# Storing each output tile by one transfer of 128 lanes in place of two of 64

## The chip, the cores and the metric

The kernel runs on one core of one Trainium2 chip. The metric is the device time of one execution in microseconds (us), the median of the runs shown. A profile of one execution on the chip, with its trace, was taken of the kernel before.

## The reference

Cosine attention over 8 batches, 12 heads, 448 positions and a head size of 64, and then a highway layer over the 3584 tokens of 768 numbers that come out of it. Inputs and output are float32.

```python
# q, k, v: (8, 12, 448, 64); tau = 0.1; w_h, w_t: (768, 768); b_t: (768,)
q_n = q / (norm(q, axis=-1) + 1e-6)
k_n = k / (norm(k, axis=-1) + 1e-6)
scores = q_n @ k_n^T / tau
attn = softmax(scores)
x = (attn @ v).transpose(0, 2, 1, 3).reshape(3584, 768)
H = maximum(x @ w_h, 0)
T = sigmoid(x @ w_t + b_t)
out = T * H + (1 - T) * x
```

## The kernel before, in words

**Layout.** The 448 positions of a batch are written as 64 lanes l by 7 positions j, position = 7 l + j (`(l j)` with `NJ = 7`). The two halves of the 128 lanes of a tile hold two different values of something: two heads of a pair in q and k, and two neighbouring j in x and in the output. The tile `x` of a batch is [128 lanes, 7, 384] and holds the attention's result in fp16.

**Attention.** For each batch, q and k are loaded (`ld_qk`, q from the SP queue at L321 and L323, k from POOL), squared (L388) and summed for the norms, scaled (`scale`, L440, mostly on POOL), and turned so that the head size lies on the lanes: by TensorE (L455) in the early batches, and by DMA transposes on SP in the later ones (q from batch 3 on at L457, k from batch 5 on at L463). `scores` makes the products (L504, L515) and their exponentials on ACT (L510, L517); `attend` multiplies by v (L529, L534, L542) and DVE divides by the sums into `x` (L550).

**Highway layer.** `ffn(b, i)` handles one of four tiles of a batch, numbered g = 4 b + i. Tiles i = 0, 1, 2 hold 128 rows of 768 numbers: lanes 0 to 63 are the rows with j = 2 i, lanes 64 to 127 those with j = 2 i + 1. The tile i = 3 (the tail) holds j = 6 alone: its 64 rows are cut into two halves of 384 numbers, one on each half of the lanes. The tile of x is turned (from batch 1 on by a DMA transpose on SP, L670, into one of five `xT` buffers), multiplied with both weights (L690, for the tail L687), put through the bias (L719), the gate (L732, L734), the product with the gate, and the last sum (L760, on POOL for most tiles), which writes the float32 tile `os`. There are four `os` buffers. `store` then writes it to the output from SP, at L770 for a whole tile and at L767 for a tail. The last two tiles (g = 30 and 31, `late`) have a path of their own with stores at L750 and L752, one half from SP and one from ACT.

**Order.** Nothing is scheduled at run time. Each piece of work is an `op` with an engine, the names that it reads, writes and uses; `ORDER` is a list of the 1911 operation numbers in the order in which they are given out, and each engine runs its own operations in that order. `SLOTS` says for each ring of buffers which buffer each new tile takes. So SP runs 109 operations in a fixed row: q loads (`ldq`), transposes of x (`xd6`, `xd3`), q (`xd7`) and k (`xdk`), and stores (`st`). One operation `st` issues two transfers. An operation that waits (a store for its `os` tile, a transpose for its source) holds all that comes behind it on SP.

Of the kernel before, what the change touches and what calls it, by code (L numbers as in the profile page):

```python
# [93 lines left out]
""".split()  # L94
)

SLOTS = {
    "qr": "01010101",
    "kr": "0120121",
    "kn": "012012012012120120120120",  # L100
    "vr": "01010101",
    "vp": "01010101",
    "sq": "012102102121021021021201012201010221021201210102",
    "n2": "01010101",
    "y": "01201201",
    "tu": "01010101010",
# [93 lines left out]
def kernel(  # L200
# [11 lines left out]
    nc = tc.nc  # L212
# [663 lines left out]
```

## Time and profile before

| what | us |
|---|---|
| median of 3 runs (lowest 250.49, highest 251.38) | 250.71 |
| profiled execution, its own time | 251.74 |
| span of the profiled execution, first to last instruction | 250.0 |
| TensorE busy (matmuls) in the span | 232.6 |
| ACT busy | 211.0 |
| DVE busy | 205.2 |
| POOL busy | 183.7 |

The profile is of one execution. Its page lists each engine's busy time, the span in 40 slices (busy tenths of each engine and of the 16 DMA engines, and the GB/s that they moved), the DMA queues (q1 is SP's, q0 is POOL's, q10 is ACT's), the chain of work that ended last, the costliest groups of instructions, and the DMA issues by tile with their size and the median time from issue to landing. A group is named by line, engine and tiles, as in "L770 SPq DMA_DIRECT2D out_dram<-os". "SPq" is SP's sequencer, which issues transfers; its issue time is not the time that the transfer takes. "DMA share" is the mean busy share of the 16 DMA engines over a stretch; it can pass 1, since the records of two queues on one engine may overlap.

### The profile page before, as it was taken

To read this page: it belongs to the slowest core of one execution; us is meant where nothing else is said; L and a number is where in the kernel's file an instruction comes from. 1 tells how busy PE (TensorE), PEld (TensorE's weight loads), DVE (VectorE), ACT (ScalarE), POOL (GpSimd) and SP (SyncE) were. 2 spreads that over 40 slices of the span, in tenths; PEclk is the share of its full clock that TensorE was granted. 3 is DMA by queue.
4 is the path that set the end of the run, shared out by engine and by line. 5 is a ranking of instruction groups with operands and counts; after the bars stand their busy time and mean duration, and the time that the engine had idled before them with its cause. 6 is when DMAs were issued, how large, how long until landed. Compare 5 with 4: busy or idle time off the path is not lost.

```text
span 250.0 us, 7394 instructions
## 1 busy us (share of the span) xinstructions
PE 232.6 (93%) x2856; PEld 147.4 (59%) x2856; DVE 205.2 (82%) x462; ACT 211.0 (84%) x421; POOL 183.7 (73%) x261
## 2 busy tenths in 40 slices
PE   7668899999999999999999999999999799999990
PEld 2246676566765765657566566656565456575650
DVE  6777899999999899999899875899974564766993
ACT  4588999999999999999999999999999399652320
POOL 8476689989989979898679778779489940334550
PEclk9855999999999999999999999999999999999996
DMA  7999999999779999999899997999996978458475
GB/s 229 296 229 271 302 248 210 198 224 210 112 132 268 167 155 239 177 134 277 257 143 175 213 151 144 247 250 161 143 174 133 181 149 185 82 143 173 121 186 157
DMA packets 75924, 47.78 MB, mean 191 GB/s; under 512 B 51568, under 2 KB 72688, under 8 KB 75888
## 3 DMA queue, kind: packets, MB, share of 16 engines
q1 hardware_dynamic: 55584, 33.86, 62.1%
q0 software_dynamic: 19856, 12.68, 39.0%
q10 hardware_dynamic: 448, 0.75, 0.9%
q8 instruction: 22, 0.36, 0.6%
q14 instruction: 14, 0.11, 0.1%
HBM read 38.34 MB, written 11.01 MB: 197 GB/s over the span
## 4 chain that ended last, share of the span: by engine, by line
PE 65%; ACT 18%; DVE 3%; DMA 3%; issue 2%; SPq 0%; DVEq 0%; ACTq 0%
PE B L690 32%; ACT E L510 10%; PE B L504 8%; PE B L534 7%; PE B L687 4%; ACT sq L388 3%; PE B L529 3%; DMA kT<-kn 3%; PE B L515 2%; PE B L455 2%; PE B L542 2%; ACT Et L517 2%; ACT E L594 2%; ACT tt L732 1%; PE B L608 1%
## 5 line engine op out<-in xcount | busy, mean ns | idle before, releaser
L510 ACT ACTIVATE E<-B 128x448 f16<-128x448 f32 x252 | 122.9, 634 | 4.6 <-PE B L504 4.5
L690 PEld LDWEIGHTS <-xT 128*128 128x128 f16 x576 | 52.6, 98 | 37.3 <-issue 7.3
L760 POOL TENSOR_TENSOR os<-x,hm 128x384 f32<-128x384 f16 x53 | 47.6, 912 | 31.5 <-DVE hm L755 19.6
L690 PE MATMUL B<-wt,xT 128*128 128x384 f16 x288 | 56.5, 326 | 0.1
L440 POOL TENSOR_TENSOR kn<-kr,y 128x192 f16<-128x192 f16 (+1 forms) x84 | 45.5, 561 | 14.7 <-DVE hm L755 6.6
L690 PE MATMUL B<-wh,xT 128*128 128x384 f16 x288 | 55.7, 326 | 0.1
L399 DVE TENSOR_REDUCE n<-sq 128x14 f32<-128x896 f32 (+1 forms) x50 | 51.1, 1037 | 3.4 <-ACT sq L388 3.2
L440 POOL TENSOR_TENSOR qn<-qr,y 128x448 f16<-128x448 f32 x47 | 43.9, 940 | 5.0 <-ACT sq L388 2.4
L732 ACT ACTIVATE tt<-z 128x768 f16<-128x768 f32 (+1 forms) x32 | 26.5, 830 | 15.9 <-DVE z L719 15.9
L534 PE MATMUL B<-vp,E 128*128 128x65 f16 x756 | 37.7, 193 | 0.0
L728 DVE SCALAR_TENSOR_TENSOR hm<-B,x 128x384 f16<-128x384 f32 x53 | 28.2, 549 | 10.2 <-PE B L690 5.5
L534 PEld LDWEIGHTS <-E 128*128 128x128 f16 x756 | 33.4, 97 | 3.0
L504 PE MATMUL B<-qT,kT 64*128 64x448 f16 x252 | 34.2, 353 | 0.0
L517 ACT ACTIVATE Et<-B 128x448 f16<-128x448 f32 x42 | 26.2, 643 | 3.6 <-PE B L515 3.5
L529 PE MATMUL B<-vp,Et 128*128 128x130 f16 x126 | 28.0, 222 | 0.0
L719 DVE TENSOR_TENSOR z<-B,bias 128x384 f32<-128x384 f32 x48 | 25.8, 545 | 2.4 <-PE B L690 2.1
L550 DVE SCALAR_TENSOR_TENSOR x<-B,rd 128x448 f16<-128x448 f32 x42 | 25.8, 618 | 0.8
L388 ACT ACTIVATE sq<-qr 128x896 f32<-128x896 f32 (+1 forms) x24 | 24.3, 1045 | 0.7 <-DMA qr<-in_q_dram 0.7
L344 POOL DMA_DIRECT2D vr<-in_v_dram x32 | 22.2, 701 | 0.1
L594 ACT ACTIVATE E<-B 128x384 f16<-128x384 f32 (+1 forms) x42 | 20.2, 644 | 1.2 <-PE B L587 1.1
L549 DVE RECIPROCAL rd<-B 128x7 f32<-128x7 f32 x42 | 8.2, 198 | 14.9 <-PE B L534 8.2
L388 ACT ACTIVATE sq<-kr 128x896 f32<-128x896 f16 x17 | 17.0, 1052 | 0.0
(79 smaller groups left out, 306.4 us busy)
## 6 DMA issues: line engine op xcount, KB each, us to landing
out_dram<-os SPq DMA_DIRECT2D x47, 192.0 KB, 3.4
qr<-in_q_dram SPq DMA_DIRECT2D x6, 1344.0 KB, 8.4
kr<-in_k_dram POOLq DMA_DIRECT2D x7, 672.0 KB, 7.9
vr<-in_v_dram POOLq DMA_DIRECT2D x16, 192.0 KB, 6.4
vr<-in_v_dram POOLq DMA_DIRECT2D x16, 144.0 KB, 6.5
qr<-in_q_dram SPq DMA_DIRECT2D x5, 448.0 KB, 7.9
out_dram<-os SPq DMA_DIRECT2D x15, 96.0 KB, 2.3
wt<-in_moe_w_t_dram POOLq DMA_DIRECT2D x1, 1152.0 KB, 13.8
```

Source lines behind the costliest of these rows:

```text
L388: nc.scalar.activation(dst, src, AF.Square, scale=sc)
L399: nc.vector.reduce_sum(R("n2", b)[:, c : c + 7 * n], a, axis=AX.X)
L440: ENG[eng].tensor_mul(N[:, :, t, :] if nm == "q" else N[:, lo > 0 : (lo > 0) + 2 * (hi - lo) - 1 : 2, t, :], source(nm, b, g)[:, t, 64 * l ...
L504: nc.tensor.matmul(R("B", ("S", n, c, t))[:, 0:S], lhsT=R("kT", i)[ln, s, 128 * c : 128 * c + 128], rhs=queries(ln), start=True, stop=True)
L510: nc.scalar.activation(R("E", n)[:, at : at + 7, :].rearrange("l j x -> l (j x)"), R("B", ("S", n, c, t))[:, 0:S], AF.Exp)
L517: op("ACT", f"expt {n}", lambda: nc.scalar.activation(R("Et", n).rearrange("l j x -> l (j x)"), R("B", ("St", n))[:, 0:S], AF.Exp), r=[("B ...
L529: nc.tensor.matmul(U[:, 2 * c : 2 * c + 2, :], lhsT=Et[:, 2 * c : 2 * c + 2, :].rearrange("l j x -> l (j x)"), rhs=vp[:, 6:8, 0:65], start ...
L534: nc.tensor.matmul(U[:, 2 * c + t, :], lhsT=E[:, at : at + 2, :].rearrange("l j x -> l (j x)"), rhs=vp[:, 3 * t + m, 0:65], start=False, s ...
L690: nc.tensor.matmul(P[:, 0:MH], lhsT=xT[:, cc, :], rhs=w_[:, cc, MH * mh : MH * mh + MH], start=(cc == 0), stop=(cc == CC - 1))
L728: op("DVE", f"hm {g} {mh}", lambda at=at, sl=sl, mh=mh: nc.vector.scalar_tensor_tensor(out=R("hm", g)[:, sl], in0=R("B", at)[:, 0:MH], sca ...
L732: op("ACT", f"th{nb} {g}", lambda: nc.scalar.activation(R("tt", g)[:, 0:W], R("z", g)[:, 0:W], AF.Tanh, scale=0.5), r=[("z", g), ("t0",)], ...
L760: op(eng, f"out {g} {mh}", lambda sl=sl, mh=mh: ENG[eng].tensor_add(R("os", g)[:, sl], xpart(mh), R("hm", g)[:, sl]), r=[("gg", g), xk], w ...
```

## The change

`store` issues one transfer for a tile in place of two. For a whole tile, the destination is both j together, `rows[2 * i : 2 * i + 2]`, whose three dimensions are j, l and m, and the source all 128 lanes. For a tail, the destination is the 64 rows with their two halves of 384 numbers put first. `rows` is a view of the output in the order j, l, m.

```diff
         def store():
             rows, O = out[b * S : b * S + S].rearrange("(l j) m -> j l m", j=NJ), R("os", g)
             if tail:
-                for h in range(2):
-                    nc.sync.dma_start(rows[6, :, MH * h : MH * h + MH], O[64 * h : 64 * h + 64, 0:MH])
+                nc.sync.dma_start(rows[6].rearrange("l (h m) -> h l m", h=2), O[:, 0:MH])
             else:
-                for h in range(2):
-                    nc.sync.dma_start(rows[2 * i + h], O[64 * h : 64 * h + 64, :])
+                nc.sync.dma_start(rows[2 * i : 2 * i + 2], O[:, :])
         op("SP", f"st {g}", store, r=[("os", g)], w=[("o", g)])
```

The two lists are exchanged as well, `ORDER` and ten of the rings of `SLOTS`. The operations and their number are the same. On SP, 16 of the 109 operations stand elsewhere, by one or two places; on PE 280 of 669, by at most 8; on ACT 163 of 425, by at most 7; on DVE 98 of 452 and on POOL 85 of 256, by at most 4. The first line of each list shows the kind of difference:

```diff
 ORDER = tuple(
...
-1 7 30 28 6 4 27 31 20 13 32 29 12 0 36 37 38 302 10 3 2 33 305 35 308 48 25 44 15 34 42 46 19 49 45 309 9 16 43 47 58
...
+30 6 7 28 4 1 27 31 20 32 29 37 36 38 302 0 3 2 33 305 35 308 48 44 34 42 46 19 49 45 309 9 16 43 47 10 58 13 12 25 15
...
```

The path of the last two tiles (`late`) stays as it was.

More of the change, by code (lines that the diff above doesn't have):

```diff
@@ L99 @@
     "kr": "0120121",
-    "kn": "012012012012120120120120",
+    "kn": "012012012012120120120102",
     "vr": "01010101",
     "vp": "01010101",
-    "sq": "012102102121021021021201012201010221021201210102",
+    "sq": "012102102121021020120210102211010221020212021210",
     "n2": "01010101",
@@ L109 @@
     "kT": "01230123013201302130213",
-    "E": "012012012012012020102012010201020120210210210210201210120",
-    "Et": "012021102101210210210210201020210102120210",
-    "rd": "010010101010101011010101010101010101010101010101010010",
+    "E": "012012012012012021012102101210121021201210210210201210120",
+    "Et": "012021102101210210210210210121201012021201",
+    "rd": "010100101010101010101010101010101010101010101010101101",
     "x": "012012012",
-    "xT": "01234012340124310234103241203214",
-    "z": "01001010101010010011010101000101",
-    "tt": "01001010101010101011010010101011",
+    "xT": "01234012340124310234103241203210",
+    "z": "01010101010101101100101010111010",
+    "tt": "01001010101010101011001101010100",
     "hm": "01210120210120121012001201210210",
-    "os": "01231020212101013213230201321023",
+    "os": "01231020212010103203213230120321",
     "B": (
-        "0123456701234567012345601273512463057134025347061351674326513027356473103247065213465072615342054627"
-        "6534207124310564516725340127632174063415602734167301243605172430547126724031547320423146750325610764"
-        "1230571640532146507314625702675013461045214736241370645320716572430173567215036504237012365714032675"
-        "1405416723504501605243676543025620154736017524315704327610534716230547603127530716452610437125604712"
-        "0562571034650731764025372146305430176451302740563270172365170345167302163540317564236147350621305276"
-        "4315362407315645123406172136504137260714356217406"
+        "0123456701234567012345670123570234567124705234716231720657316405627136243071452063403675012345620453"
+        "7421503652460176147351260453760325467231460572345674053267150436740512516034715630163412570364720572"
+        "1360451723406527413074163526513270450127620345620431351064721637540236413721064105367027541325067431"
+        "2650156340721054670512434012570375061423651740271652043671503674502317420653706251473165426371054630"
+        "5173160524716470620453165704123012764301725432760541254607135427130451673425730642174203745612573014"
+        "2656240173652415206174230625471620317240651374021"
     ),
```

144 rows, old and new, of the table ORDER are left out of this document.

## The prediction

> **What bounds the kernel now.** I read the page first: its span, the busy shares, the slices, the DMA queues and the chain.
>
> ```profile
> span 250.0 us, 7394 instructions
> PE 232.6 (93%) x2856; PEld 147.4 (59%) x2856; DVE 205.2 (82%) x462; ACT 211.0 (84%) x421; POOL 183.7 (73%) x261
> DMA  7999999999779999999899997999996978458475
> GB/s 229 296 229 271 302 248 210 198 224 210 112 132 268 167 155 239 177 134 277 257 143 175 213 151 144 247 250 161 143 174 133 181 149 185 82 143 173 121 186 157
> q1 hardware_dynamic: 55584, 33.86, 62.1%
> q0 software_dynamic: 19856, 12.68, 39.0%
> q10 hardware_dynamic: 448, 0.75, 0.9%
> PE 65%; ACT 18%; DVE 3%; DMA 3%; issue 2%; SPq 0%; DVEq 0%; ACTq 0%
> ```
>
> TensorE is busy for 93% of the span and carries 65% of the chain; the sequencer SP, which issues the stores, carries 0%. That is the first reading: a store is off the path, and fewer store issues can hardly buy anything. The second reading is the DMA line: in most slices the sixteen DMA engines are at seven to nine tenths or more, though they move only 112 to 302 GB/s. These engines are shared by everything, and nearly full as an average. So the question that decides is not how many transfers are issued but how evenly the bytes lie on the sixteen engines.
>
> Next, the issues by tile, to see what the changed lines do and when.
>
> ```profile
> L770 SPq DMA_DIRECT2D out_dram<-os x46: 467/588/1392, 74.9 to 243.6; - x46
> L767 SPq DMA_DIRECT2D out_dram<-os x14: 541/582/598, 99.1 to 230.5; - x14
> DMA to landing us min/median/max: 2.2/3.2/8.5
> out_dram<-os SPq DMA_DIRECT2D x47, 192.0 KB, 3.4
> out_dram<-os SPq DMA_DIRECT2D x15, 96.0 KB, 2.3
> qr<-in_q_dram SPq DMA_DIRECT2D x6, 1344.0 KB, 8.4
> ```
>
> L770 issues 46 halves of whole tiles, 192 KB each, and L767 14 halves of tail tiles, 96 KB each: 23 whole tiles and 7 tails, the first at 74.9 us. The last two tiles (L752, L750) are not touched.
>
> **The change, part by part.**
>
> *Issues.* Thirty of the 60 issues at 0.588 and 0.582 us go: 30 x 0.587 = 17.6 us of SP's time. SP is on no share of the chain, so I cost this at nothing; what it could be worth at most is the first rival.
>
> *What one transfer now looks like.* Before, both sides of a store count 64 lanes first: 64 rows of 3072 bytes, lane after lane in the tile, 21,504 bytes apart in the output. After, the tile side counts 128 lanes, but the output side cannot: lanes 0 to 63 go to rows of j = 2i and lanes 64 to 127 to the same rows of j = 2i + 1, and j steps by 3072 bytes where l steps by 21,504. So the 128 rows are no single series; the destination is two halves of 64, the halves outermost. The tails are alike (two halves of 64 rows of 1536 bytes, 1536 bytes apart). The q load looks like a counter-example, since its source is also written with a two outermost (s = 2), and it lands 1344 KB in 8.4 us, which no two engines could do: 1344 KB / 8.4 us = 164 GB/s. It isn't one: its s step is 64 times its l step (448 rows of 64 numbers against 7 of them), so those lanes do fold into one series of 128. Every transfer of the profile that I followed in the code counts 64 or 128 first on both sides. No row shows an outermost count under sixteen, so the cost is bounded from both sides: spread over sixteen engines as now, it is nothing or a small gain; shared out by the halves, one engine takes one half, and two engines carry all the output of 30 tiles. I take two engines, because the halves are the only outer count in which lanes of the tile and rows of the output agree without cutting a half. The Trainium skill says this outright: in "DMA: Bandwidth & Descriptors", section "Why a DMA increments its semaphore by 16 and not by 1", the number of engines is the largest up to 16 that divides the slowest dimension of both access patterns, which would be 2 for 128 and 2, and 16 for the 64 and 64 of before. The q load's 164 GB/s agrees with it, as its folded 128 gives 16; the case of 2 is shown by no row here.
>
> *The price on an engine.* A whole tile puts 64 rows of 3072 bytes, 0.1966 MB, on each of the two engines; a tail half that.
>
> ```profile
> core 0: us, PE busy (x) PEld busy (x) DVE busy (x) ACT busy (x) POOL busy (x), PEclk, DMA share, GB/s
> 75.00:208.00 133.00, 131.00 (x1609) 81.34 (x1606) 110.82 (x244) 126.50 (x258) 107.73 (x153) 1.00 1.10 186
> 208.00:250.00 42.00, 35.75 (x378) 22.52 (x375) 28.46 (x67) 17.09 (x33) 14.21 (x16) 0.95 0.64 152
> 235.30:235.60 0.30, 0.30 (x4) 0.17 (x3) 0.30 (x1) 0.00 (x0) 0.30 (x2) 1.00 1.08 420
> ```
>
> The last row is a piece in which a store alone runs on full engines: 420 GB/s at a share of 1.08 is 420 / (16 x 1.08) = 24.3 GB/s for one engine. The q10 row of the page, loads and the last stores with the pauses between, gives 0.75 MB in 0.9% of 16 x 250 us = 36 us, or 20.8. Two engines with 64 rows queued on each are full, so the 420 row is nearest: 0.1966 MB / 24.3 GB/s = 8.1 us for a whole tile and 4.05 for a tail, where the store now lands in 3.4 and 2.3. At 20.8 it would be 9.45 and 4.7. The ends of the rate are 20.8 and 26.2 (420 / 16, not divided by the share).
>
> *The sum.* These stores do not spread over the run. The timeline of SP shows where they bunch:
>
> ```profile
> 207.96 2.50 SPq L770 DMA_DIRECT2D out_dram<-os  x4
> 210.56 2.90 SPq L670 DMA_TRANSPOSE xT<-x  x2
> 213.51 1.22 SPq L767 DMA_DIRECT2D out_dram<-os  x2
> 219.34 3.18 SPq L770 DMA_DIRECT2D out_dram<-os  x4
> 223.35 3.87 SPq L670 DMA_TRANSPOSE xT<-x  x3
> 227.28 1.22 SPq L767 DMA_DIRECT2D out_dram<-os  x2
> 228.59 1.19 SPq L770 DMA_DIRECT2D out_dram<-os  x2
> 229.88 1.18 SPq L767 DMA_DIRECT2D out_dram<-os  x2
> 231.16 1.24 SPq L670 DMA_TRANSPOSE xT<-x  x1
> 232.50 11.71 SPq L770 DMA_DIRECT2D out_dram<-os  x10
> ```
>
> From 208 us on there are 2 + 2 + 1 + 5 = 10 whole tiles and 3 tails; before it 13 and 4. Up to 75 us nothing changes: 75 us. From 75 to 208 the two engines must do the stores, 13 x 8.1 + 4 x 4.05 = 121.5 us, and their sixteenth of all else. All else is 186 GB/s x 133 us = 24.7 MB, less 13 x 0.393 + 4 x 0.197 = 5.9 MB of stores, so 18.8 MB, 1.18 MB for one engine. Its rate lies between that of the two large queues together (46.5 MB in 101.1% of 4000 us, 11.5 GB/s) and that of q1 alone (33.86 MB in 62.1%, 13.6 GB/s); at 12.5 it is 94 us. That stage takes 215 us in place of 133 if the two engines never pause. From 208 us the stores are 10 x 8.1 + 3 x 4.05 = 93 us and all else 152 x 42 = 6.4 MB less 5.1 MB of stores (the last two tiles' among them), 0.08 MB for one engine, 6 us: 99 us in place of 42. With about 3 us until the last lands, as now (3.4), the two engines alone need 75 + 215 + 99 + 3 = 392 us.
>
> They will pause. What waits behind a store: in SP's queue the DMA transposes of xT, qT and kT and the q loads, which need all engines and so also these two; on SP itself the next store, which waits for its tile; on POOL the sum of L760, which waits for one of four `os` buffers, and behind it the scaling of the next batch's q and k (L440), which SP transposes. If nothing of a store's 8.1 us lay beside other work, the middle stage would take its 133 us plus 121.5 less what its stores cost now on sixteen engines (5.9 MB / 16 / 24.3 = 15 us), 239 us. That is 24 us over 215; four `os` buffers let two or three tiles queue while TensorE goes on, so I take a third, 8 us. 400 us of span. The profiled execution took 251.74, 1.74 outside its span, and lies 1.03 above the median of 250.71: 400 + 1.74 - 1.03 = 401 us.
>
> *The new order.* The lists are written anew: PE's and ACT's operations trade places with near neighbours, 16 of SP's 109 move by one or two. The instructions stay the same, so the busy times stay; it moves waits in both directions, within the 17 us in which PE isn't busy (250.0 - 232.6), most of which lie at the start and end. I take nothing, within 2.5 us either way.
>
> **The rivals.**
>
> *Spread over sixteen engines after all*, by folding inside the hardware or because the lowering cuts the transfer in two again. Then only SP's time falls, and it decides where a transpose waits behind stores. The chain shows one such place:
>
> ```profile
> 191.50 0.53 SPq L457
> 192.09 6.41 DMA kT<-kn
> kT<-kn SPq DMA_TRANSPOSE x18, 4.7
> ```
>
> A kT that lands at its median saves 6.41 - 4.7 and at most the issue before it, 0.53: 2.2 us, so 248.5 us, or nothing if the transfer is cut again, 250.7. For it: 0.59 us for an issue is real, and SP issues two for each tile. Against it: the destination doesn't fold. The Trainium skill speaks for it as well, on the same page, section "Rules for kernel authors": two transfers to disjoint halves of the lanes share the same engines anyway, and one of 128 lanes is advised. Which of the page's two rules wins is the case's question; the destination's halves settle it for me. Chance 0.10: 0.05 for the gain, 0.04 for no change, 0.01 for a small loss by the new order.
>
> *Two engines, and no overlap at all*: each store holds up all that comes behind it, SP's transposes first, so TensorE stands still for each. The middle stage is then the 239 us from above, and the last one 42 + 93 less the 12 us that its stores cost now (4.5 MB / 16 / 24.3), 123: 75 + 239 + 123 = 437 us of span, 438 us. With 20.8 in place of 24.3 the three terms are 75, 257 and 137, which makes 470. It decides if a transpose is needed sooner behind a store than 8 us after its issue; they land in 4.7 us and the chain has 3% of DMA waits now, so some are. Chance 0.2.
>
> *Two engines, but less to carry*: at 26.2 GB/s and with all else at 13.6 GB/s and no pauses, 75 + (113 + 86) + (86 + 6) + 3 = 369 us. It is the lower end of the forecast.
>
> **How the numbers follow.** Two engines with most of the overlap, 369 to 430 us: 0.70, and the likeliest is 401. No overlap: 0.20, 430 to 470. Sixteen engines: 0.10, about 250. The range from 368 to 466 leaves out the sixteen and the far end of the second case, under 2 in 10. About 0.5% can be told from no change here: faster 0.05, same 0.04, slower 0.91.
>
> **What would show it.** Right: 23 issues of 384 KB and 7 of 192 KB, landing in over 8 and 4 us, most of them far more behind one another; slices in which only stores run fall to about 50 GB/s (2 x 24.3) at a DMA share of about one tenth (2 of 16); the DMA `out_dram<-os` and DMA transposes have a large share of the chain and PE falls under 60% of the span with the same busy time, though its granted clock may fall in the pauses; the last transposes issue after 290 us and the end is a run of stores. The packets keep number and size: the q1 row keeps its bytes and grows in packets only by what completions differ. Wrong: stores that land in about 3.4 us, or a last stage that still moves 150 GB/s, mean that the engines are shared out otherwise, and the time is then about that of before. If the time is slower but under 368 us, the two engines carry less than I gave them; if it is over 466, the transposes' waits, not the engines, set the pace.

## The result and the profile after

The changed kernel takes 395.19 us (median of 6 runs, 394.0 to 396.39) against 250.54 us (6 runs): a ratio of 1.5775, 95% interval 1.5744 to 1.5806. The profiled execution took 394.75 us with a span of 393.0 us. The prediction was 401 us, range 368 to 466. In what follows, where the runs of one kernel lay over 1.5% apart (n8 and the two merged ones from POOL's queue), the time given is the median of the faster ones.

The page of the changed kernel, in the parts shown of before: span, engines, granted clock, slices of the DMA engines, SP's queue, the chain and the store's own rows.

```profile
span 393.0 us, 7325 instructions
PE 263.5 (67%) x2856; PEld 160.2 (41%) x2856; DVE 206.6 (53%) x462; ACT 213.8 (54%) x421; POOL 183.9 (47%) x261
PEclk9659999999869897879959995895967977786555
DMA  9999999889999798994969999959795919222131
GB/s 238 258 246 233 206 203 188 125 209 79 71 176 147 105 62 77 234 100 88 63 121 210 113 70 82 148 64 90 112 91 75 64 56 74 71 56 72 52 87 44
q1 hardware_dynamic: 54684, 33.86, 63.5%
DMA 43%; PE 17%; ACT 13%; POOL 7%; SPq 5%; issue 4%; DVE 1%; DVEq 0%; POOLq 0%; ACTq 0%
DMA out_dram<-os 31%; ACT E L510 7%; PE B L690 7%; DMA qr<-in_q_dram 4%; DMA xT<-x 3%; DMA qT<-qn 3%; PE B L504 3%; POOL os L760 3%; ACT sq L388 2%; SPq L457 2%; SPq L463 2%; POOL kn L440 2%; PE B L534 2%; ACT E L594 2%; DMA kT<-kn 1%
out_dram<-os SPq DMA_DIRECT2D x23, 384.0 KB
out_dram<-os SPq DMA_DIRECT2D x8, 192.0 KB
```

The engines' work is the same in count, and DVE's, ACT's and POOL's busy times moved by under 3 us. TensorE's rose by 31 us, which comes up again below; the rest is time around the work. TensorE, 65% of the chain before, has 17%, and the store alone has 31%; it was not on the chain of before. Two readings say how many engines carry a store. First, q1 moves the same 33.86 MB, but in 900 packets fewer, 54684 for 55584. Two transfers on sixteen engines end with 32 completion packets; if one transfer on k engines ends with k, 30 tiles save 30 x (32 - k), and 900 gives k = 2. (The runs below bear the counting out: n4 has 54744 packets, 30 x 28 fewer, and n8 54864, 30 x 24 fewer.) Second, a stretch near the end in which nothing but stores is in flight, below the two stages in which the prediction made its sum (columns: the stretch, busy time and instructions of each engine, granted clock, share of the sixteen DMA engines, GB/s):

```profile
core 0: us, PE busy (x) PEld busy (x) DVE busy (x) ACT busy (x) POOL busy (x), PEclk, DMA share, GB/s
75.00:295.00 220.00, 154.72 (x1643) 90.28 (x1642) 114.47 (x249) 131.61 (x264) 110.15 (x155) 0.85 1.15 114
295.00:393.00 98.00, 45.85 (x394) 27.49 (x391) 28.90 (x67) 17.82 (x34) 14.65 (x16) 0.69 0.43 65
362.00:372.00 10.00, 0.00 (x0) 0.00 (x0) 0.00 (x0) 0.00 (x0) 1.88 (x3) 0.50 0.13 52
```

In the last row a share of 0.13 is two engines of sixteen (0.125), and 52 GB/s is 26 for each. The other fourteen stand still, and TensorE runs no matmul.

The two rows of output issues carry no time to landing, nor do any of SP's other transfers on the page. The trace's records of the semaphores, which count what has landed, give it when they are paired with the issues in order (the last section says how): a whole tile lands 10.2 to 25.5 us after its issue, 14.7 in the median, and a tail 6.5 to 17.3, 11.2 in the median. A transpose of x lands in 10.5 in the median, where the kernel before has 3.7. What waited shows it as well. From the list of waits (us in all, times, longest):

```profile
POOL os L760 <- DMA out_dram<-os: 101.8, 19, 10.7
ACT E L510 <- PE B L504: 56.3, 23, 9.4
DVE hm L728 <- POOL os L760: 33.3, 7, 9.7
PE B L690 <- DMA xT<-x: 18.5, 6, 7.2
PE B L504 <- DMA qT<-qn: 10.8, 3, 6.3
```

POOL waits 102 us for an `os` buffer that a store hasn't left yet; DVE waits for POOL, TensorE for transposes, which SP issues in one row with the stores, and ACT for TensorE. The end on SP's timeline is a run of stores, held back by the `os` tiles that POOL can't write:

```profile
337.42 8.62 SPq L670 DMA_TRANSPOSE xT<-x  x1
346.13 26.59 SPq L768 DMA_DIRECT2D out_dram<-os  x5
372.82 7.54 SPq L752 DMA_DIRECT2D out_dram<-os  x1
```

### The profile page after: what moved, and what is told of

It reads as the page before. It is cut to its first block, busy times and chain, and to the rows that moved or that the text cites. A ratio compares the mean times of both kernels' runs of the same rounds, so it can differ in the third digit from the quotient of the medians.

```text
span 393.0 us, 7325 instructions
## 1 busy us (share of the span) xinstructions
PE 263.5 (67%) x2856; PEld 160.2 (41%) x2856; DVE 206.6 (53%) x462; ACT 213.8 (54%) x421; POOL 183.9 (47%) x261
## 3 DMA queue, kind: packets, MB, share of 16 engines
q1 hardware_dynamic: 54684, 33.86, 63.5%
## 4 chain that ended last, share of the span: by engine, by line
DMA 43%; PE 17%; ACT 13%; POOL 7%; SPq 5%; issue 4%; DVE 1%; DVEq 0%; POOLq 0%; ACTq 0%
DMA out_dram<-os 31%; ACT E L510 7%; PE B L690 7%; DMA qr<-in_q_dram 4%; DMA xT<-x 3%; DMA qT<-qn 3%; PE B L504 3%; POOL os L760 3%; ACT sq L388 2%; SPq L457 2%; SPq L463 2%; POOL kn L440 2%; PE B L534 2%; ACT E L594 2%; DMA kT<-kn 1%
## 5 line engine op out<-in xcount | busy, mean ns | idle before, releaser
L690 PEld LDWEIGHTS <-xT 128*128 128x128 f16 x576 | 55.1, 103 | 62.3 <-DMA xT<-x 19.8
L690 PE MATMUL B<-wt,xT 128*128 128x384 f16 x288 | 63.1, 352 | 16.3 <-DMA xT<-x 15.8
L690 PE MATMUL B<-wh,xT 128*128 128x384 f16 x288 | 61.9, 347 | 2.8 <-DMA xT<-x 2.7
L504 PE MATMUL B<-qT,kT 64*128 64x448 f16 x252 | 39.8, 387 | 35.5 <-DVE hm L728 18.1
L440 POOL TENSOR_TENSOR qn<-qr,y 128x448 f16<-128x448 f32 x47 | 43.8, 937 | 30.7 <-DVE tt L734 17.3
L534 PE MATMUL B<-vp,E 128*128 128x65 f16 x756 | 40.9, 200 | 0.0
L534 PEld LDWEIGHTS <-E 128*128 128x128 f16 x756 | 36.5, 103 | 4.2 <-ACT E L510 0.9
L529 PE MATMUL B<-vp,Et 128*128 128x130 f16 x126 | 29.3, 233 | 0.7 <-ACT E L510 0.7
L504 PEld LDWEIGHTS <-kT 64*128 64x128 f16 x252 | 9.7, 96 | 42.4 <-issue 29.7
L687 PEld LDWEIGHTS <-xT 128*64 128x64 f16 x180 | 12.4, 135 | 32.9 <-DMA xT<-x 16.5
L687 PE MATMUL B<-wt,xT 128*64 128x384 f16 x96 | 12.7, 402 | 16.5 <-DMA xT<-x 15.3
```

The costliest lines, as they stand in the source:

```text
L440: ENG[eng].tensor_mul(N[:, :, t, :] if nm == "q" else N[:, lo > 0 : (lo > 0) + 2 * (hi - lo) - 1 : 2, t, :], source(nm, b, g)[:, t, 64 * l ...
L504: nc.tensor.matmul(R("B", ("S", n, c, t))[:, 0:S], lhsT=R("kT", i)[ln, s, 128 * c : 128 * c + 128], rhs=queries(ln), start=True, stop=True)
L529: nc.tensor.matmul(U[:, 2 * c : 2 * c + 2, :], lhsT=Et[:, 2 * c : 2 * c + 2, :].rearrange("l j x -> l (j x)"), rhs=vp[:, 6:8, 0:65], start ...
L534: nc.tensor.matmul(U[:, 2 * c + t, :], lhsT=E[:, at : at + 2, :].rearrange("l j x -> l (j x)"), rhs=vp[:, 3 * t + m, 0:65], start=False, s ...
L690: nc.tensor.matmul(P[:, 0:MH], lhsT=xT[:, cc, :], rhs=w_[:, cc, MH * mh : MH * mh + MH], start=(cc == 0), stop=(cc == CC - 1))
```

## The experiments

Two theories were on trial. **C** (capacity): the bytes on two engines set the pace. **W** (waits): each step that needs all sixteen engines waits for the slowest of them, whether or not there is room in total. The rivals from outside are the new order, the form of 128 lanes in itself, and the place and step of the rows. Times of the kernel before beside these runs were 250.18 to 250.33 us.

| kernel | store of a tile | engines | us | ratio, 95% |
|---|---|---|---|---|
| changed | one, 2 x 64 rows | 2 | 395.2 | 1.5744 to 1.5806 |
| e1_order | two of 64 lanes, new order | 16 | 251.6 | 1.0044 to 1.0072 |
| e2_store | as changed, old order | 2 | 392.1 | 1.5603 to 1.5729 |
| n2 | one, outermost 2, rows together | 2 | 398.8 | one run |
| n4 | one, outermost 4 | 4 | 310.7 | 1.2349 to 1.2487 |
| n8 | one, outermost 8 | 8 | 264.7 | 1.0536 to 1.0595 |
| n16 | one, outermost 16 | 16 | 251.6 | 1.0042 to 1.0068 |
| n16_old | as n16, old order | 16 | 250.6 | 0.9997 to 1.0031 |
| e6_tails | only tails merged | 2 for tails | 267.5 | 1.0645 to 1.0774 |
| os8 | as changed, eight `os` buffers | 2 | 399.3 | 1.5877 to 1.5997 |
| p128 | as changed, from POOL | 2, moving | 372.8 | 1.4840 to 1.4961 |
| p128_os8 | the same, eight `os` buffers | 2, moving | 357.3 | 1.4208 to 1.4318 |
| p64 | two of 64 lanes, from POOL | 16 | 267.6 | 1.0641 to 1.0712 |

**The order or the transfer.** One kernel takes the new lists alone, one the merged stores alone.

```diff
 # e1_order: against the changed kernel
-                nc.sync.dma_start(rows[2 * i : 2 * i + 2], O[:, :])
+                for h in range(2):
+                    nc.sync.dma_start(rows[2 * i + h], O[64 * h : 64 * h + 64, :])
...
 # e2_store: against the kernel before
-                for h in range(2):
-                    nc.sync.dma_start(rows[2 * i + h], O[64 * h : 64 * h + 64, :])
+                nc.sync.dma_start(rows[2 * i : 2 * i + 2], O[:, :])
...
```

> The new order and buffer lists, with each tile stored by two transfers of 64 lanes as before. Theory (a merged transfer runs on two of the sixteen DMA engines): the order costs nothing, 250.7 us within 2.5 either way, out_dram issues 46 x 192 KB and 14 x 96 KB, q1 packets 55584. Rival (the new order makes the time): about 395 us.

> The old order and buffer lists, with the merged stores alone. Theory (two engines): 385 to 405 us, q1 packets 54684, which is 900 fewer: 30 x (2 x 16 - 2) completion packets. Rival (the order): about 251 us. If the plan of the new lists hides part of the cost, this run is slower than the changed kernel's 395.

The lists alone make 0.58%, 1.4 us; the merged stores alone 392.1 us (two runs), with q1 at the same 54684 packets. The loss is the transfer's. The plan of the new lists hides none of it.

**The number of engines.** The same one transfer of 128 lanes from SP, with only the count outermost in the destination changed. These kernels leave out the order of the output's rows: each tile goes to rows that lie together, and the last two tiles go where room is left, so their output is not the reference's.

```diff
-                nc.sync.dma_start(rows[2 * i : 2 * i + 2], O[:, :])
+                t = 3 * b + i
+                nc.sync.dma_start(out[128 * t : 128 * t + 128].rearrange("(r a) m -> a r m", a=16), O[:, :])
 # a = 2, 4, 8, 16; tails alike in 64 rows from 3072 + 64 * b on; n16_old: the old lists
```

> The changed kernel, each tile still stored by one transfer of 128 lanes from SP, but to a destination whose outermost count is 16: a whole tile goes to 128 rows that lie together, row 16 r + a for lane 8 a + r, so the output's rows are permuted (the last two tiles go where room is left, by their own path). Theory (the outermost count of the destination sets the number of engines): 16 engines, 251 us within 2.5, q1 packets 55584 - 30 x 16 = 55104. Rival (one transfer of 128 lanes is slow in itself, or what waits behind it): about 395 us.

> As n16 with an outermost count of 2: row 2 r + a for lane 64 a + r, in the same block of 128 rows, so the row step inside a half is 6144 bytes and not 21504. Output rows permuted in the same way. Theory (two engines, the step does not matter): 385 to 405 us, q1 packets 54684. Rival (the 21504-byte steps or the permuted place make the time): about 251 us.

> As n16 with an outermost count of 8 (output rows permuted in the same way). Theory: eight engines carry the stores, 10.42 MB / 8 = 1.30 MB each, 54 us at 24.3 GB/s. From 75 to 208 us such an engine has 94 us of other work and 30 us of stores, 124 of 133, and from there 6 + 23 of 42, so it still fits: 251.6 us as n16 up to 256 with pauses. Rival (any count under sixteen stalls the transposes behind a store): 270 us or more.

> As n16 with an outermost count of 4 (output rows permuted in the same way). Theory: four engines, 2.61 MB of stores each, 107 us. From 75 to 208 us such an engine has 94 + 61 = 155 us for 133, then 6 + 46 = 52 for 42: 75 + 155 + 52 + 3 = 285, with pauses 285 to 305 us. Rival (time in proportion to the landing of a store, all of it on the path): half of the 147 us that n2 lost against n16, about 325.

> The old order and buffer lists, one transfer of 128 lanes for each tile on sixteen engines (outermost count 16, output rows permuted as in n16). It prices the halved issues alone, 17.6 us of SP's time. The prediction's rival gave 248.5 us at best; as SP is not on the chain, 250.2 us within 0.5% is expected, and the 0.55% of n16 is then the new order's.

With sixteen outermost the transfer of 128 lanes costs what two of 64 cost (251.6 and 251.6 with the new lists). Its rows, from the page of n16:

```profile
q1 hardware_dynamic: 55104, 33.86, 63.0%
out_dram<-os SPq DMA_DIRECT2D x23, 384.0 KB, 4.8
out_dram<-os SPq DMA_DIRECT2D x8, 192.0 KB, 3.3
```

480 completion packets fewer than before are 30 x (32 - 16), and the landing times are back. So neither the one transfer nor its 128 lanes is slow; with two outermost, in the same block of rows, it is 398.8 us, and the step of 21,504 bytes is cleared too, as n2's is 6144. This is the rule that the prediction drew from the Trainium skill ("DMA: Bandwidth & Descriptors", "Why a DMA increments its semaphore by 16 and not by 1"), and the case of 2 now has its trace. The Trainium skill's other rule on the same page, in "Rules for kernel authors", one transfer of 128 lanes in place of two halves, did not hold for this destination.

In n16_old the 30 issues saved are worth nothing that can be told from no change (1.0014, 0.9997 to 1.0031).

But theory C was out for n8 and n4. It allowed n8 at most 256 us, as an engine there has room for its bytes; 264.7 was measured, 13 more than n16. n4 came to 310.7 against 285 to 305. W's price, all of the longer landing on the path, was given as 270 or more and about 325. Both lie between. C's sums also take each stage as a whole: n8's engines were to be busy for 124 us of 133, so bytes that bunch within a stage could overload them for a while without any step of W. No run parts the two.

**Few slow stores with some room to spare.** By C's sum the two engines are busy for 123 us of the 133 up to 208 us.

```diff
 # e6_tails: against the changed kernel
-                nc.sync.dma_start(rows[2 * i : 2 * i + 2], O[:, :])
+                for h in range(2):
+                    nc.sync.dma_start(rows[2 * i + h], O[64 * h : 64 * h + 64, :])
```

> The new lists, with only the seven tails merged (two engines), the whole tiles by two transfers of 64 lanes. Theory (capacity of the two engines): 94 + 13 + 4 x 4.05 = 123 of the 133 us up to 208, and under 42 after it, so most is hidden: 251.6 to 256 us. Rival (each merged store holds up what is behind it): 251.6 + 7 x (4.05 - 0.5) = 276 us.

267.5 us: 16 us above e1_order for seven transfers, 2.3 us for each, where C allowed 4.4 in all and W said 24. It fits neither. Its chain by lines, and two of its waits:

```profile
PE B L690 16%; ACT E L510 10%; DMA out_dram<-os 8%; DMA xT<-x 6%; PE B L534 5%; PE B L504 5%; ACT sq L388 3%; ACT E L594 3%; DMA kT<-kn 3%; PE B L687 3%; POOL kn L440 2%; PE B L529 2%; PE B L542 2%; PE B L455 2%; ACT Et L517 2%
```

```profile
POOL os L760 <- DMA out_dram<-os: 18.0, 7, 4.2
PE B L690 <- DMA xT<-x: 6.6, 2, 5.3
```

Stores and transposes of x are on the chain, 8% and 6%, though the two engines had room over the stage. Room in total didn't hide a slow store whose buffer or engine was needed next; whether the engines were full just then is open here too.

**More buffers.**

```diff
-    "os": "01231020212010103203213230120321",
+    "os": "01234567102564170564327051437620",
...
-        os=(4, [128, DM], FP32), B=(8, [128, 512], FP32))
+        os=(8, [128, DM], FP32), B=(8, [128, 512], FP32))
```

> The changed kernel with eight os buffers in place of four. Theory C (the bytes on the two engines set the pace, which are busy nearly all the time): 385 to 395 us, the pauses alone go, and POOL's 102 us of waits for os buffers move to the transposes and the end. Theory W (what counts is the wait of each later step for one slow transfer, and the os buffers are the worst of these waits): most of the 102 us go, 300 to 350 us.

399.3 us, 1% over the changed kernel and 4 us over the range that C gave; W's 300 to 350 is out. The largest wait, 102 us of POOL for `os` buffers, is gone from the list, and the time isn't shorter. The waits of os8 that a DMA ended, longest first, and its chain by lines:

```profile
PEld L690 <- DMA xT<-x: 29.5, 7, 10.7
PE B L690 <- DMA xT<-x: 27.9, 7, 10.3
PE B L504 <- DMA qT<-qn: 20.2, 3, 14.7
```

```profile
DMA xT<-x 30%; PE B L690 13%; DMA kT<-kn 6%; DMA qr<-in_q_dram 5%; ACT E L510 4%; PE B L504 3%; PE B L534 3%; PE B L687 3%; SPq L457 2%; ACT sq L388 2%; ACT E L594 2%; PE B L529 1%; POOL qn L440 1%; PE B L542 1%; PE B L515 1%
```

The transposes of x have taken the place of the stores, 30% of the chain for 31%. A queue that is too long can be waited for at its end or at its start. With two engines for all the output, C comes closest: the wait changed its place, and the time didn't fall.

**Another pair for each store.** The same merged transfer, and the two halves as a control, from POOL's queue.

```diff
-                nc.sync.dma_start(rows[2 * i : 2 * i + 2], O[:, :])
+                nc.gpsimd.dma_start(rows[2 * i : 2 * i + 2], O[:, :])
...
-        op("SP", f"st {g}", store, r=[("os", g)], w=[("o", g)])
+        op("POOL", f"st {g}", store, r=[("os", g)], w=[("o", g)])
```

> The changed kernel with the merged stores issued from POOL's queue in place of SP's, right behind the sums that POOL makes. The transfer still has two halves outermost. If the two engines are always the same two (theory as first put, two full engines): 385 to 400 us, as only SP's queue gets free. If the pair goes round from transfer to transfer, which the Trainium skill says of this queue (DMA: Bandwidth & Descriptors, Why a DMA increments its semaphore by 16 and not by 1): a store still takes 8 us, but the engines share the bytes, and the time is 255 to 275 us, part of it for 30 issues of about 0.7 us on POOL (21 us of its 66 us of idle time).

> The merged stores from POOL's queue, with eight os buffers. If the pair of engines goes round there (store traffic passed two engines' 51 GB/s in places of the run before), the total of bytes leaves room: theory C then expects a clear fall from 378, to under 330, as more stores can run side by side. Theory W: the os waits go (56 us), but each transpose still needs all sixteen engines and lands behind the slowest, 12.7 us in place of 3.7: 340 to 375 us.

> The new order with two transfers of 64 lanes for each tile as before, but issued from POOL's queue. Control for the move to POOL: sixteen engines, 60 issues of about 0.8 us on POOL (48 us). If the move itself is not what made 378 us: 252 to 275 us. If it is: 350 us or more.

The Trainium skill says, in "DMA: Bandwidth & Descriptors", section "Why a DMA increments its semaphore by 16 and not by 1", that from POOL's queue a transfer on fewer than sixteen engines takes its engines in turn. The trace agrees as far as it goes: near the end of p128_os8, with all transposes long issued, stores move 89 GB/s on a share of 0.28, about four and a half engines, where the pair of the changed kernel had 52. So more than one pair works at once; which engines they are, the trace doesn't name. The page gives landing times again here. The stretch, the issues and the chain of p128_os8:

```profile
336.00:338.00 2.00, 1.50 (x27) 0.97 (x24) 1.99 (x5) 0.46 (x1) 1.70 (x3) 1.00 0.28 89
```

```profile
out_dram<-os POOLq DMA_DIRECT2D x23, 384.0 KB, 15.9
xT<-x SPq DMA_TRANSPOSE x28, 12.8
kT<-kn SPq DMA_TRANSPOSE x18, 9.3
qT<-qn SPq DMA_TRANSPOSE x15, 12.0
```

```profile
DMA xT<-x 24%; PE B L690 14%; ACT E L510 7%; DMA qT<-qn 7%; DMA kT<-kn 3%; PE B L504 3%; PE B L687 3%; SPq L457 3%; PE B L534 2%; ACT sq L388 2%; ACT E L594 2%; SPq L463 2%; POOL kn L440 1%; PE B L455 1%; ACT Et L517 1%
```

With no fixed pair to be overloaded the time fell to 372.8, and to 357.3 with eight buffers. The forecast for p128 with a pair that moves, 255 to 275, was about 100 us too low, and C's under 330 for p128_os8 was missed as well; W's 340 to 375 held. The transposes of x, still from SP and on all engines, land in 12.8 us, and are 24% of the chain. From the issues of the kernel before and of p64, in this order:

```profile
xT<-x SPq DMA_TRANSPOSE x28, 3.7
xT<-x SPq DMA_TRANSPOSE x28, 4.5
```

p64 took 267.6 us, so the move to POOL costs 16 us, and the two engines of each store the other 105 of p128. This is what W says: a store that is slow on any two engines makes the transfers over all sixteen late. How two queues share the packets of one engine was not tried alone.

## Why the prediction was right

*Two engines, by the outermost count.* Right, and now shown in four ways: 900 packets, a share of 0.13, the row from n2 to n16, and the semaphore records in the last section.

*The rate.* 24.3 GB/s for an engine was taken. Where stores run alone 26 was measured (52 / 2), near the upper end that was given, 26.2. Over the whole run the records of the stores' own packets in the trace give 23.3 in the mean and 25.4 in the median, so some packets are slower; that they share an engine with other transfers just then is likely and not shown. 24.3 was a fair size.

*The sum.* Forecast: 75 + 223 + 102 = 400 us of span, with 8 us of pauses in the middle. The last stage begins in the changed kernel with the store at 294.98 us, from where 10 whole tiles and 3 tails remain: 75, 220 and 98. Each stage is within 4 us. The stores' packets took 125 us of each of the two engines in the middle stage and 96 in the last, where 121.5 and 93 were forecast. In the middle stage that leaves some 95 us for all else and the pauses together, where 94 + 8 were forecast.

*What the pauses are.* This stays open. At 26 GB/s for the stores the two engines would need 75 + (94 + 113) + (6 + 87) + 3 = 378 us without a pause, and 15 us of the span would be pauses; at 23.3, which counts shared time twice, the sum is 402 us, more than the whole span. The 94 us of all else was an estimate that no run measured by itself, and the third taken for the pauses was a choice, so that the total came within 2% is in part luck. What the neighbours show is that the prediction's reason for small pauses, that two or three queued tiles hide most of a slow store, doesn't carry over to engines with some room: n8 cost 13 us, where C left at most 4, and seven tails 16. Total bytes fit the changed kernel, whose two engines are overloaded, and not its neighbours.

*The issues at nothing, the new order at nothing within 2.5 us.* Right: 0.14%, not told from zero, and 1.4 us.

*The rivals.* Sixteen engines and a gain: didn't come about, and n16_old shows that even then there is none: the 6.41 us wait for a kT is not on its chain, and its time is no shorter. No overlap at all, 438: too much by 43 us; a part of each slow store does lie beside other work.

*The signs.* 23 and 7 issues, 50 GB/s at a tenth, the same bytes on q1, the run of stores at the end: as said, and so are the landing times from the semaphore records, none under 10.2 us for a whole tile. PE under 60% with the same busy time was wrong: it is 67%, since the same 2856 matmuls took 263.5 us for 232.6. The mean granted clock fell from 0.965 to 0.815, and the L690 matmuls from 326 ns to about 350:

```profile
L690 PE MATMUL B<-wt,xT 128*128 128x384 f16 x288 | 63.1, 352 | 16.3 <-DMA xT<-x 15.8
L690 PE MATMUL B<-wh,xT 128*128 128x384 f16 x288 | 61.9, 347 | 2.8 <-DMA xT<-x 2.7
```

I read that as a consequence of the pauses: the granted clock was 1.00 from 75 to 208 us of the kernel before, with TensorE busy for 131 us of 133, and 0.50 in the stretch above without a matmul. No run holds the clock fixed, so its part in the time is not shown.

No version that beats both kernels came out of this. One transfer for each tile with the output's rows in their places and sixteen engines would need the lanes in another order, and wasn't tried.

## What to carry to other kernels

Before merging two transfers, write down the dimensions of both sides as they fold, and look at the outermost count: from SP's queue it decided here how many engines carry the bytes. A leading 2 cost 145 us, and thirty issues saved were worth nothing. Check it in the profile by the DMA share in a stretch where only that transfer runs, and by the completion packets. Don't count on room over a whole stage: with eight engines, busy for 124 us of 133 by the estimate, the price was already 13 us.

## What the runs showed of the hardware that was not expected

The page gives no time to landing for any transfer of SP's queue in the changed kernel, and in n4 and n8 alike. It gives it again in n16, in the kernels that store from POOL, and in e6_tails for part of the transfers. The trace's records of the semaphores show why. A transfer over all engines leaves 16 updates of its semaphore; each merged store of the changed kernel leaves 3, and each store of n8 leaves 9. The page pairs sixteen updates with each issue, and where the count doesn't come out it gives no time for any transfer that uses the same semaphore. In the changed kernel eight semaphores are short by 390 updates, 13 for each of the 30 stores. So in these two kernels k engines leave k + 1 updates: one early, in the changed kernel 0.9 to 9.6 us after the issue, and k later, the last of them taken here as the landing. The Trainium skill says, in "DMA: Bandwidth & Descriptors", section "Why a DMA increments its semaphore by 16 and not by 1", that the sequencer itself writes the missing 16 - k counts at once when only k engines carry a transfer. The one early update agrees with that; who writes it, the trace doesn't tell.

A DMA transpose can hold SP for longer than its issue. For those of x in the kernel before and then in the changed kernel, the least, median and longest hold in ns:

```profile
L670 SPq DMA_TRANSPOSE xT<-x x28: 1211/1269/2462, 70.0 to 231.2; - x28
L670 SPq DMA_TRANSPOSE xT<-x x28: 1178/2758/10597, 73.1 to 337.4; - x28
```

In n16, with the lists of the changed kernel and stores on sixteen engines, the median is 1268. So the long holds come with the slow stores, and SP's next issues are late too, though a whole tile's own issue takes 0.52 us in the median. What a transpose waits for while it holds SP is not shown.
